# Blocks of four rows per partition for w2, the bias added on VectorE, and the tail rows of w2 on the load queue

## The chip, the cores and the metric

The kernel runs on one core of a Trainium2 chip. The metric is device time in microseconds (us), the median of several executions.

The engines go by their names in the profile: PE is TensorE's matmul and PEld its weight load, DVE is VectorE, ACT ScalarE, POOL GpSimd, and SP is SyncE, which issues most of the loads. The DMA engines carry a load in packets; it has *landed* when its semaphore, a counter that others wait on, has counted all of it. SBUF is the on-chip memory, 128 partitions, into which the loads write.

Two kinds of number appear. *Times* come from unprofiled executions, with a 95% interval on the ratio to the kernel before, run on the same chip. *Trace numbers* come from one profiled execution of each kernel; its span is about 2 us shorter than the time. A trace number has no interval, so differences of 0.2 us between two traces are not read as anything. Packet durations, landings and addresses that stand in no profile view were counted from the packet and semaphore records of the traces and from the built programs.

## The reference

A decode step: one token for each of four sequences goes through attention over a cache of 4096 positions, then through a small MLP.

```python
# x [4,1,640]; k_cache, v_cache [4,32,4096,128]; wq [640,4096]; wo [4096,640]
# w1 [640,1728]; b1 [1728]; w2 [1728,640]; all bf16
h  = x + attention(layernorm(x), k_cache, v_cache, wq, wo)
t  = layernorm(h) @ w1 + b1
sp = log1p(exp(-abs(t))) + where(t > 0, t, 0)
out = h + (t * tanh(sp)) @ w2
```

The two caches are 268 MB of the 283 MB read. The MLP weights, which the change is about, are 4.4 MB.

## The kernel before

P is 128 partitions, D is 640, F is 1728. F is FM = 13 full blocks of 128 and FT = 64 rest rows. DC = 5 is the number of 128-blocks in D, N = 4 the sequences, FC = 14 the blocks of F with the rest, CG = 4. One pool of four slots of 32 KB per partition takes the whole stream in turn: wq, then 64 cache tiles of 4 MB (key and value tiles, alternating), then half of wo, then w1.

```python
consts = ctx.enter_context(tc.tile_pool(name="consts", bufs=1))
stream = ctx.enter_context(tc.tile_pool(name="stream", bufs=NSLOT))     # NSLOT = 4
...
def load_cache(store, src, i, nm, parts=1):
    hg, b = tiles[i]
    t = stream.tile([P, SLOT], BF16, tag="s", name=f"{nm}{i}")          # SLOT = 16384: 32 KB
    view = src[b, hg * G : (hg + 1) * G].rearrange("h (q r) d -> (h q) (r d)", q=PG)
    n = SLOT // parts
    for k in range(parts):
        nc.sync.dma_start(out=t[:, k * n : (k + 1) * n], in_=view[:, k * n : (k + 1) * n])
...
w2_sb = consts.tile([P, FM, D], BF16)
W1S = (0, 2, 4, DC)
W2S = (0, 5, 10, FM)
def load_mlp():
    w1_slot = stream.tile([P, SLOT], BF16, tag="s", name="w1_slot")
    ...                                     # w1 in three loads, by W1S
    w2_v = B_w2[0 : FM * P, :].rearrange("(p j) n -> p j n", j=FM)      # partition p has rows 13p..13p+12
    for j0, j1 in zip(W2S, W2S[1:]):
        nc.sync.dma_start(out=w2_sb[:, j0:j1, :], in_=w2_v[:, j0:j1, :])
...
b1T = consts.tile([P, FM + 1], BF16)
nc.scalar.dma_start(out=b1T[:, 0:FM], in_=B_b1[0 : FM * P].rearrange("(p j) -> p j", j=FM))
nc.scalar.dma_start(out=b1T[0:FT, FM : FM + 1], in_=B_b1[FM * P : F].rearrange("(p o) -> p o", o=1))
...
ident_f = consts.tile([P, P], FP32)         # 512 bytes a partition
...
if i == 0:                                  # in the loop over cache tiles: the tail rows, mid-stream
    nc.scalar.dma_start(out=w2_tail[0:FT, :], in_=B_w2[FM * P : F, :])
    nc.scalar.dma_start(out=w2_tail[FT : FT + CG, :], in_=B_w2[F - CG : F, :])
...
b1s = consts.tile([P, FC, N], FP32)         # b1 times std; 224 bytes a partition
...
for c0, c1 in zip(W1S, W1S[1:]):
    if c1 == DC:                            # the bias, by an fp32 matmul with the identity
        nc.tensor.matmul(h1_ps[:, :, :], lhsT=ident_f[:, :], rhs=b1s[:, :, :], start=False, stop=False)
    for j in [FM] + list(range(FM)):
        for c in range(c0, c1):
            # column j of w1 for partition p is column 13p + j: 13 columns, 26 bytes, apart
            ...
            nc.tensor.matmul(h1_ps[0 : (P if j < FM else FT), j, :], lhsT=w, rhs=cen[:, c, :], ...)
# h1 = h1_ps * rstd, mish on ScalarE and VectorE -> act; then act @ w2_sb and act @ w2_tail
```

A weight tile of w1 is the stationary operand, so its columns are read by the weight load (PEld in the profile). The order in which rows of w2 lie on the partitions sets which columns of w1 must be read together: 13 apart here.

The softmax here doesn't subtract the row's maximum and nothing guards it: scores larger than these inputs give would overflow.

## Time and profile before

| | before |
|---|---|
| time, median of the first 3 runs | 670.02 us (669.18 to 670.12) |
| span in the trace | 667.5 us |
| last wo part landed | 652.61 |
| last w2 part landed | 662.96 |
| last w2 matmul done | 664.34 |

The page's slices: 40 equal parts of the span, first the busy share of the DMA engines in tenths, then what they moved; the third line counts packets.

```profile
DMA  9999999999999999999999999999999999999995
GB/s 376 440 411 438 419 438 435 432 427 439 432 427 430 430 436 429 438 437 423 432 437 431 433 428 436 437 430 427 434 437 436 429 429 432 438 431 430 427 415 241
DMA packets 12591, 283.81 MB, mean 425 GB/s; under 512 B 1608, under 2 KB 1680, under 8 KB 3728
```

The load stream is the limit in 39 of 40 slices. PE is busy 64% and VectorE 62% of the span, so both have time to spare. Two stretches of the stream, as windows (start and end in us, length, then busy time of PE, PEld, DVE, ACT and POOL with the instruction counts, granted TensorE clock, DMA share, GB/s):

```profile
100.00:300.00 200.00, 128.60 (x890) 59.66 (x889) 127.29 (x134) 20.50 (x93) 0.00 (x0) 0.82 1.00 432
300.00:500.00 200.00, 130.28 (x828) 59.01 (x827) 129.01 (x138) 20.56 (x96) 0.00 (x0) 0.83 1.00 432
```

Only in the last 11 us, after 656.86, does the chain stop waiting for loads. The chain of waits that ended last (start, length, what; the trace prints w1's slot as w_slot, w2_sb as w_sb, the product of w1 as h_ps, that of w2 as y_ps):

```profile
641.55 15.31 DMA w_slot<-in_B_w_dram
656.86 0.04 issue
656.90 1.89 PE h_ps L537 x28
658.80 0.52 PE h_ps L528 x2
659.32 1.02 PE h_ps L537 x14
...
661.91 0.23 DVE act L576
662.14 0.04 issue
662.18 2.16 PE y_ps L585 x55
664.34 0.02 issue
664.37 0.33 DVE o_bf L591
```

After the second part of w1 has landed (656.86) the chain runs through 28 w1 matmuls in 1.89 us, the fp32 bias matmul in 0.52 us (L528), 14 more, the activation, and 55 w2 matmuls. From the timeline (start, length, engine, line, operation, and in brackets the idle time before):

```profile
656.90 1.81 PEld L537 LDWEIGHTS <-w_slot 128*64 128x64 bf16 x28 [0.28 <-DMA w_slot<-in_B_w_dram]
662.41 1.91 PE L585 MATMUL y_ps<-w_sb,act 128*4 128x160 bf16 x52
```

A group of 28 w1 matmuls is paced by its weight loads: 1.81 us of 1.89. The w2 matmuls run without a wait. In all, PE is 1.4 us behind the last load.

### The profile page before, as it was taken

To read this page: it belongs to the slowest core of one execution; us is meant where nothing else is said; L and a number is where in the kernel's file an instruction comes from. 1 tells how busy PE (TensorE), PEld (TensorE's weight loads), DVE (VectorE), ACT (ScalarE), POOL (GpSimd) and SP (SyncE) were. 2 spreads that over 40 slices of the span, in tenths; PEclk is the share of its full clock that TensorE was granted. 3 is DMA by queue.
4 is the path that set the end of the run, shared out by engine and by line. 5 is a ranking of instruction groups with operands and counts; after the bars stand their busy time and mean duration, and the time that the engine had idled before them with its cause. 6 is when DMAs were issued, how large, how long until landed. Compare 5 with 4: busy or idle time off the path is not lost.

```text
span 667.5 us, 6967 instructions
## 1 busy us (share of the span) xinstructions
PE 426.0 (64%) x2937; PEld 198.2 (30%) x2937; DVE 411.7 (62%) x477; ACT 75.5 (11%) x312; POOL 1.9 (0%) x9
## 2 busy tenths in 40 slices
PE   1967546694567675574764865568765657747586
PEld 0323222242223332232332422233322223323145
DVE  3387565686565676465675666557765657757542
ACT  0401001010001110011100110101100111001011
POOL 1000000000000000000000000000000000000000
PEclk9987789897788976788877788979867898778895
DMA  9999999999999999999999999999999999999995
GB/s 376 440 411 438 419 438 435 432 427 439 432 427 430 430 436 429 438 437 423 432 437 431 433 428 436 437 430 427 434 437 436 429 429 432 438 431 430 427 415 241
DMA packets 12591, 283.81 MB, mean 425 GB/s; under 512 B 1608, under 2 KB 1680, under 8 KB 3728
## 3 DMA queue, kind: packets, MB, share of 16 engines
q1 hardware_dynamic: 12224, 283.27, 98.8%
q8 instruction: 23, 0.38, 0.2%
q10 hardware_dynamic: 336, 0.10, 0.1%
q14 instruction: 8, 0.07, 0.0%
HBM read 283.36 MB, written 0.01 MB: 424 GB/s over the span
## 4 chain that ended last, share of the span: by engine, by line
DMA 61%; DVE 19%; PE 18%; issue 1%; ACT 0%; SPq 0%; DVEq 0%; ACTq 0%
DVE prod L284 16%; PE red L296 14%; DMA k_1005<-in_A_k_cache_dram 4%; DMA k_530<-in_A_k_cache_dram 4%; DMA k_1480<-in_A_k_cache_dram 4%; DMA k_1955<-in_A_k_cache_dram 4%; DMA k_2881<-in_A_k_cache_dram 4%; DMA k_2428<-in_A_k_cache_dram 4%; DMA k_3334<-in_A_k_cache_dram 4%; DMA k_1691<-in_A_k_cache_dram 4%; DMA k_310<-in_A_k_cache_dram 4%; DMA k_3092<-in_A_k_cache_dram 4%; DMA k_1216<-in_A_k_cache_dram 3%; DMA k_741<-in_A_k_cache_dram 3%; DMA v_3666<-in_A_v_cache_dram 3%; DMA k_2166<-in_A_k_cache_dram 3%
## 5 line engine op out<-in xcount | busy, mean ns | idle before, releaser
L296 PE MATMUL red<-prod,ident 128*128 128x512 bf16 x1024 | 300.1, 451 | 218.9 <-DVE prod L284 218.0
L296 PEld LDWEIGHTS <-ident 128*128 128x128 bf16 x1024 | 116.0, 114 | 385.2 <-issue 317.6
L313 DVE TENSOR_REDUCE s_f<-red 128x32 f32<-128x512 f32 x128 | 88.1, 688 | 79.4 <-PE red L296 79.2
L316 ACT ACTIVATE ex<-s_f 128x32 bf16<-128x32 f32 x128 | 29.3, 229 | 516.6 <-DVE s_f L313 516.6
L323 DVE TENSOR_TENSOR e<-ex,hmask 128x128 bf16<-128x128 bf16 x128 | 36.5, 285 | 6.1 <-ACT ex L316 6.1
L373 PEld LDWEIGHTS o_ps<-selo,pv_sb 128*128 128x128 f32 x256 | 34.0, 194 | 6.0 <-ACT pv_sb L363 1.2
L352 PEld LDWEIGHTS <-e 128*16 128x16 bf16 x1024 | 22.6, 89 | 36.8 <-issue 15.5
L373 PE MATMUL o_ps<-selo,pv_sb 128*128 128x4 f32 x256 | 31.1, 245 | 0.7 <-ACT pv_sb L363 0.7
L316 ACT ACTIVATION_READ_ACCUMULATOR ex<-s_f 128x1 f32 x128 | 23.9, 187 | 0.1
L284 DVE TENSOR_TENSOR prod<-k_79,qbc 128x4096 bf16<-128x4096 bf16 x4 | 9.1, 2287 | 17.6 <-DMA k_79<-in_A_k_cache_dram 17.6
L379 DVE TENSOR_TENSOR OT<-o_ps,rl 128x16 bf16<-128x16 f32 x8 | 1.6, 195 | 21.0 <-PE o_ps L373 21.0
L256 PE MATMUL q_ps<-wq_74,lnT 128*4 128x512 bf16 x32 | 10.7, 470 | 4.7 <-DMA wq_74<-in_A_wq_dram 4.7
L284 DVE TENSOR_TENSOR prod<-k_1691,qbc 128x4096 bf16<-128x4096 bf16 x4 | 9.1, 2286 | 5.7 <-DMA k_1691<-in_A_k_cache_dram 5.7
L284 DVE TENSOR_TENSOR prod<-k_3092,qbc 128x4096 bf16<-128x4096 bf16 x4 | 9.1, 2286 | 5.7 <-DMA k_3092<-in_A_k_cache_dram 5.7
L284 DVE TENSOR_TENSOR prod<-k_1216,qbc 128x4096 bf16<-128x4096 bf16 x4 | 9.1, 2286 | 4.9 <-DMA k_1216<-in_A_k_cache_dram 4.9
L284 DVE TENSOR_TENSOR prod<-k_3545,qbc 128x4096 bf16<-128x4096 bf16 x4 | 9.1, 2286 | 4.9 <-DMA k_3545<-in_A_k_cache_dram 4.9
L284 DVE TENSOR_TENSOR prod<-k_741,qbc 128x4096 bf16<-128x4096 bf16 x4 | 9.1, 2285 | 4.9 <-DMA k_741<-in_A_k_cache_dram 4.9
L284 DVE TENSOR_TENSOR prod<-k_903,qbc 128x4096 bf16<-128x4096 bf16 x4 | 9.1, 2287 | 4.8 <-DMA k_903<-in_A_k_cache_dram 4.8
L284 DVE TENSOR_TENSOR prod<-k_428,qbc 128x4096 bf16<-128x4096 bf16 x4 | 9.1, 2286 | 4.6 <-DMA k_428<-in_A_k_cache_dram 4.6
L284 DVE TENSOR_TENSOR prod<-k_1378,qbc 128x4096 bf16<-128x4096 bf16 x4 | 9.1, 2286 | 4.5 <-DMA k_1378<-in_A_k_cache_dram 4.5
L284 DVE TENSOR_TENSOR prod<-k_1853,qbc 128x4096 bf16<-128x4096 bf16 x4 | 9.1, 2286 | 4.5 <-DMA k_1853<-in_A_k_cache_dram 4.5
L284 DVE TENSOR_TENSOR prod<-k_530,qbc 128x4096 bf16<-128x4096 bf16 x4 | 9.1, 2285 | 4.4 <-DMA k_530<-in_A_k_cache_dram 4.4
(179 smaller groups left out, 376.2 us busy)
## 6 DMA issues: line engine op xcount, KB each, us to landing
wq_74<-in_A_wq_dram SPq DMA_DIRECT2D x1, 4096.0 KB
k_79<-in_A_k_cache_dram SPq DMA_DIRECT2D x1, 4096.0 KB, 24.8
k_81<-in_A_k_cache_dram SPq DMA_DIRECT2D x1, 4096.0 KB, 33.9
v_83<-in_A_v_cache_dram SPq DMA_DIRECT2D x1, 4096.0 KB, 17.3
k_244<-in_A_k_cache_dram SPq DMA_DIRECT2D x1, 4096.0 KB
v_246<-in_A_v_cache_dram SPq DMA_DIRECT2D x1, 4096.0 KB
k_310<-in_A_k_cache_dram SPq DMA_DIRECT2D x1, 4096.0 KB, 24.6
v_314<-in_A_v_cache_dram SPq DMA_DIRECT2D x1, 4096.0 KB, 32.1
```

What stands on the lines that cost most here:

```text
L256: nc.tensor.matmul(q_ps[:, :], lhsT=lnT[:, c, :], rhs=wq_t[c // WQC][:, o : o + 512], start=(c == 0), stop=(c == DC - 1),)
L284: nc.vector.tensor_tensor(out=t[:, :, :], in0=kt[i][:, s * RS : (s + 1) * RS, :], in1=q_bc[hg][:, b, :].unsqueeze(1).to_broadcast([P, RS, ...
L296: nc.tensor.matmul(red[:, :, :], lhsT=ident[:, :], rhs=t[:, :, c * CW : (c + 1) * CW], start=(c == 0), stop=(c == Dh // CW - 1),)
L313: nc.vector.tensor_reduce(out=s_t[i][:, sl], in_=reds.pop((i, s))[:, :, :], axis=AX.X, op=ALU.add)
L316: nc.scalar.activation(out=ex_t[i][:, sl], in_=s_t[i][:, sl], func=ACT.Exp, scale=SCALE, accum_out=rs_t[hg][:, b, s : s + 1],)
L323: nc.vector.tensor_tensor(out=e_t[i][:, sl, :], in0=ex_t[i][:, sl].unsqueeze(2).to_broadcast([P, RS, G]), in1=hmask[:, :].unsqueeze(1).to_ ...
L352: nc.tensor.matmul(pvs[i % 2][k * QD : k * QD + RQ * G, :], lhsT=e_t[i][:, u * RQ : (u + 1) * RQ, :], rhs=vt[i][:, u * RQ : (u + 1) * RQ, ...
L373: nc.tensor.matmul(o_ps[hg][:, b, :], lhsT=t[:, r, :], rhs=selo[:, r, :], start=(r == 0), stop=(r == RQ - 1),)
L379: nc.vector.tensor_tensor(out=OT[:, hg * G : (hg + 1) * G, :].rearrange("p g b -> p b g"), in0=o_ps.pop(hg)[:, :, :], in1=rl.pop(hg)[:, :] ...
```

## The change

The intent is to shorten this last stretch. Rows of w2 go in blocks of four per partition, so that the w1 columns read together are 4 apart (8 bytes) and no longer 13 (26 bytes). b1 is added by VectorE after the product, so the fp32 matmul, its identity and its scaled operand go. The tail rows of w2 leave the middle of the stream and go on the load queue, in two pieces, right before w2. b1 has to follow the new order and becomes five small loads. The core of the diff:

```diff
-    W2S = (0, 5, 10, FM)
+    JW = 4
+    EB = 8
+    def fcols(t, j):
+        if j == FM:
+            return t[:, FM * P : F]
+        j0 = j - j % JW
+        w = min(JW, FM - j0)
+        return t[:, j0 * P : (j0 + w) * P].rearrange("k (p r) -> k r p", r=w)[:, j - j0, :]
...
-        for j0, j1 in zip(W2S, W2S[1:]):
-            nc.sync.dma_start(out=w2_sb[:, j0:j1, :], in_=w2_v[:, j0:j1, :])
+        for r0, r1 in ((0, FT - EB), (FT - EB, FT)):
+            nc.sync.dma_start(out=w2_tail[r0:r1, :], in_=B_w2[FM * P + r0 : FM * P + r1, :])
+        for j in range(0, FM, JW):
+            w = min(JW, FM - j)
+            nc.sync.dma_start(out=w2_sb[:, j : j + w, :],
+                in_=B_w2[j * P : (j + w) * P, :].rearrange("(p r) n -> p r n", r=w))
...
-    nc.scalar.dma_start(out=b1T[:, 0:FM], in_=B_b1[0 : FM * P].rearrange("(p j) -> p j", j=FM))
+    for j in range(0, FM, JW):
+        w = min(JW, FM - j)
+        nc.scalar.dma_start(out=b1T[:, j : j + w],
+            in_=B_b1[j * P : (j + w) * P].rearrange("(p r) -> p r", r=w))
...
-    ident_f = consts.tile([P, P], FP32)
-    nc.vector.tensor_copy(out=ident_f[:, :], in_=ident[:, :])
...
-        if i == 0:                 # both tail loads of the cache loop go
-            ...
-    b1s = consts.tile([P, FC, N], FP32)
-    ...                            # its multiply and the fp32 matmul go
-                    h1_ps[0 : (P if j < FM else FT), j, :], lhsT=w, rhs=cen[:, c, :],
+                    h1_ps[0 : (P if j < FM else FT), j, :],
+                    lhsT=fcols(w1_sb[:, c, :], j), rhs=cen[:, c, :],
...
+    nc.vector.tensor_tensor(
+        out=h1[:, :, :], in0=h1[:, :, :],
+        in1=b1T[:, :].unsqueeze(2).to_broadcast([P, FC, N]), op=ALU.add,
+    )
```

## The prediction

> **What bounds the kernel now.** The load stream. The page's slices show the DMA engines at 9 tenths in 39 of 40 slices, 425 GB/s over 283.8 MB; DVE is 62% busy, PE 64%. The landing events in the trace follow each other every 9.66 us per 4 MB cache tile from 64 us to the end, so what shifts the stream early shifts the end. The change leaves these bytes alone: only the last 15 us and some tenths elsewhere are at stake.
>
> **The last 15 us (timeline, chain of waits).** The last output-projection weights land at 652.61. The first group of w1 matmuls starts at 654.79 (after the centred input), the second at 656.90 (its w1 landed 656.86), 28 in 1.9 us each; the third part of w1 lands at 657.90, but PE gets to it only at 659.25, after group two and the fp32 bias matmul (0.52 us on the chain). w1 product done 660.34, activation 662.13, w2 matmuls 2.16 us to 664.34. The last w2 part lands at 662.96, so loads are only 1.4 us ahead of PE.
>
> **Saved.**
> 1. w1 column stride. Successive weight loads start 60 ns apart at a 26-byte stride, 40 ns at the 10-byte stride of the first transposition, 27 ns for contiguous columns. The Trainium skill, "SBUF — State Buffer", section on the DMA port swizzle, says that SBUF has 16-byte lines and each new line costs; the three spacings agree (128, 80, 16 lines). At 8 bytes (64 lines) I estimate 30 ns: a group of 28 takes about 1.0 us.
> 2. The bias matmul goes; a DVE add of about 0.25 us comes in after the w1 product.
>
> Group two then ends near 657.9, group three waits for its DMA at 657.90 and ends about 658.4: 1.9 us earlier, less 0.25. Activation done near 660.5.
>
> **What eats it.** PE reaches w2 columns 8 to 11 before that piece has landed; the last piece (1,280-byte rows, 55 ns a packet; 196 ns for 5,120) lands at about 663.3 if nothing else moves. PE would end near 663.7: a gain of 0.6 us.
>
> **Moved.** The w2 tail rows (4 packets of 55 ns per engine) leave the middle of the stream, where between 44 and 57 us two tiles took 10.45 and 9.99 us instead of 9.66: up to 0.9 us off; at the end they cost about 0.25. b1 becomes four small loads of 128 descriptors (before: one), 9 ns a packet, 24 more per engine: about 0.25 us. Splitting the tail 56 + 8 leaves two engines free of it (The Trainium skill, "DMA: Bandwidth & Descriptors", section on why a DMA increments its semaphore by 16; no view here shows engine numbers). Net: 0 to 0.5 us gained.
>
> **Sum.** About 1.0 us less: 669.0 us, range 667.8 to 670.4. Faster by over 2%: 0.01; within 2%: 0.98; slower: 0.01.
>
> **Right or wrong shows in:** w1 weight loads about 30 ns apart, first group about 1.0 us; PE idle before the third w1 group and a late w2 group, released by DMA; the chain ending in w2's last landing; tiles between 36 and 57 us at 9.7 to 9.9 us.
>
> **What would make it wrong.** An 8-byte stride costs as much as 26; the small b1 loads hold a semaphore that a cache load or the first square root waits for, and a bubble opens near 30 us; instruction fetches (16 KB; the spread of landings jumps from 1.9 to 3.4 and 3.2 to 4.7 us near two of them) fall differently on the slowest engine.

## The result

| | before | after |
|---|---|---|
| time, median of 6 | 669.59 us (669.18 to 670.12) | 672.41 us (672.24 to 672.71) |
| span in the trace | 667.5 | 670.5 |
| last wo part landed | 652.61 | 656.10 |
| last w2 part landed | 662.96 | 666.94 |
| last w2 matmul done | 664.34 | 667.42 |

The ratio is 1.0042, with a 95% interval of 1.0029 to 1.0055. (A ratio here and below is the mean time of one kernel's fast runs over the mean of the other's in the same rounds, so it is not quite the ratio of the medians.) That is within 2%, as predicted, but the sign is wrong, and 672.41 lies outside the predicted range.

The change is about the end of the kernel, and there it did its work: from the landing of the last wo part to the last w2 matmul, before took 664.34 - 652.61 = 11.73 us and after 667.42 - 656.10 = 11.32. But wo landed 3.49 us *later*, at a point that no changed instruction of the MLP has reached. The page of after:

```profile
DMA  9999999999999999999999999999999999999996
GB/s 374 434 408 434 419 436 432 432 423 437 426 429 430 426 436 426 436 431 425 431 431 427 435 428 432 425 432 437 426 433 426 433 437 423 432 428 436 425 406 255
DMA packets 13165, 283.81 MB, mean 423 GB/s; under 512 B 2058, under 2 KB 2254, under 8 KB 4302
```

The same windows of after:

```profile
100.00:300.00 200.00, 131.26 (x886) 60.50 (x885) 126.13 (x133) 20.51 (x93) 0.00 (x0) 0.83 1.00 430
300.00:500.00 200.00, 129.99 (x818) 58.11 (x816) 127.77 (x136) 20.25 (x94) 0.00 (x0) 0.83 1.00 430
```

The DMA share is 1.00 in both kernels, so there is no bubble: the engines are as busy and move less, 430 GB/s in place of 432. Both kernels load the same cache tiles here with the same instructions. The digits are coarse; the trace's packet records are finer. Durations of the 32 KB packets of the load queue between 100 and 600 us:

```
before   1213 ns x6489 of 6524                      mean 1214.7
after    1216 ns x3584, 1224 ns x1408, 1215 x612    mean 1219.7
```

In before nearly every packet takes exactly 1213 ns. In after hardly one does. A 4 MB tile lands every 9.66 us in before and every 9.72 us in after, and 0.05 to 0.06 us on each of some 59 tiles after the first five is about 3 us.

At the end the chain of after reads:

```profile
639.81 16.29 DMA wo_late<-in_A_wo_dram
656.10 0.02 issue
656.12 10.42 DMA w_sb<-in_B_w_dram
666.53 0.04 issue
666.57 0.86 PE y_ps L589 x15
667.44 0.02 issue
667.46 0.33 DVE o_bf L595
```

It goes through w2's landing, as the prediction said it would: PE is no longer behind the loads. And the timeline of after:

```profile
658.30 1.11 PEld L536 LDWEIGHTS <-w_slot 128*64 128x64 bf16 x28 [0.27 <-DMA w_slot<-in_B_w_dram]
660.59 1.78 PEld L536 LDWEIGHTS <-w_slot 128*64 128x64 bf16 x42 [1.18 <-DMA w_slot<-in_B_w_dram]
662.74 0.22 DVE L567 TENSOR_TENSOR h_4147<-h_4147,b1T 128x56 f32<-128x56 f32 x1
666.57 0.84 PE L589 MATMUL y_ps<-w_sb,act 128*4 128x160 bf16 x20 [0.55 <-DMA w_sb<-in_B_w_dram]
```

28 weight loads take 1.11 us where they took 1.81; the added VectorE instruction costs 0.22; PE waits 0.55 us for the last of w2.

So there are two questions: why does an untouched stream move 0.5% slower, and what became of the gains the prediction had summed up?

### The profile page after: what moved, and what is told of

It reads as the page before. It is cut to its first block, busy times and chain, and to the rows that moved or that the text cites. A ratio compares the mean times of both kernels' runs of the same rounds, so it can differ in the third digit from the quotient of the medians.

```text
span 670.5 us, 6968 instructions
## 1 busy us (share of the span) xinstructions
PE 429.9 (64%) x2935; PEld 198.2 (30%) x2935; DVE 410.9 (61%) x476; ACT 75.5 (11%) x312; POOL 1.9 (0%) x9
## 4 chain that ended last, share of the span: by engine, by line
DMA 64%; DVE 19%; PE 16%; issue 0%; ACT 0%; DVEq 0%
DVE prod L301 16%; PE red L313 14%; DMA k_1004<-in_A_k_cache_dram 4%; DMA k_1479<-in_A_k_cache_dram 4%; DMA k_529<-in_A_k_cache_dram 4%; DMA k_1954<-in_A_k_cache_dram 4%; DMA k_2880<-in_A_k_cache_dram 4%; DMA k_2427<-in_A_k_cache_dram 4%; DMA k_3333<-in_A_k_cache_dram 4%; DMA k_309<-in_A_k_cache_dram 4%; DMA v_3546<-in_A_v_cache_dram 4%; DMA k_3091<-in_A_k_cache_dram 4%; DMA k_1690<-in_A_k_cache_dram 4%; DMA k_79<-in_A_k_cache_dram 4%; DMA k_2165<-in_A_k_cache_dram 3%; DMA k_1215<-in_A_k_cache_dram 3%
## 5 line engine op out<-in xcount | busy, mean ns | idle before, releaser
L313 PE MATMUL red<-prod,ident 128*128 128x512 bf16 x1024 | 306.4, 459 | 215.7 <-DVE prod L301 214.7
L313 PEld LDWEIGHTS <-ident 128*128 128x128 bf16 x1024 | 117.9, 116 | 385.8 <-issue 321.2
```

Of the source, the lines that this page charges most:

```text
L313: nc.tensor.matmul(red[:, :, :], lhsT=ident[:, :], rhs=t[:, :, c * CW : (c + 1) * CW], start=(c == 0), stop=(c == Dh // CW - 1),)
```

## The experiments

What the change could have done to the whole stream: it removed two scratch tiles, `ident_f` (512 bytes a partition) and `b1s` (224), from the pool of constants that lies below the stream's slots. The addresses in the built programs:

```
before         slots start at 57600 = 225 * 256
after          slots start at 56864 = 222 * 256 + 32     (736 bytes lower)
```

**ADDRESS**: the slots' start, no longer a multiple of some power of two, slows every large packet. **BIAS**, the rival: the five small b1 loads in place of two disturb the stream, by a semaphore or a queue state that lasts. The expectations name a third theory, **TAIL**: the tail rows on the other queue in mid-stream had kept the stream of before out of the slow pattern. It falls with before_pad32, which keeps them there and is slow, and with after_pad224, which does not and is fast. Each experiment below changes the kernel named and is compared with before on the same chip.

### A. The start address

**A1. 32 bytes of padding in the kernel before** (and, A2, in the kernel after). The pad is a tile that nothing reads.

```diff
     w2_tail = consts.tile([P, D], BF16)
+    pad = consts.tile([P, 16], BF16, name="pad")
+    nc.gpsimd.memset(pad[:, :], 0.0)
```

Expected of the kernel before with the pad:

> The kernel before with nothing but a 32-byte tile put among the constants, so that the stream buffers start 32 bytes off a multiple of 64. ADDRESS: packets 1216 to 1224 ns, a cache tile every 9.72 us, about 3.5 us slower: 673 us. BIAS and TAIL: 1213 ns and 669.6 us.

Measured: 673.23 us (673.06 to 673.42), ratio 1.0053 (1.0038 to 1.0068). Its windows:

```profile
100.00:300.00 200.00, 130.07 (x886) 60.17 (x885) 126.14 (x133) 20.52 (x93) 0.00 (x0) 0.84 1.00 430
300.00:500.00 200.00, 129.32 (x818) 57.80 (x817) 127.76 (x136) 20.25 (x94) 0.00 (x0) 0.84 1.00 430
```

430 GB/s, and the packets are those of after: 1216 ns x3595, 1224 ns x1401, mean 1219.7. The kernel before, with nothing of the change in it, is made slow by 32 bytes that no one reads. This alone is larger than the whole result.

Expected of the kernel after with the pad:

> The changed kernel is slower because every 32 KB packet of the load stream takes 1216 to 1224 ns from about 75 us on, against 1213 ns before. Theory ADDRESS: taking away two scratch tiles moved the stream buffers from a start that is a multiple of 64 bytes to one that is 32 off; a pad of 32 bytes puts it back: packets 1213 ns to the end, a cache tile every 9.66 us, 668.5 to 669.5 us, so about 1 us under the kernel before. Theory BIAS (the four small b1 loads put the stream into the slow pattern) and theory TAIL (the tail rows on the second queue at 40 us had kept it out of it): no difference, 1216 to 1224 ns, 672.4 us.

Measured: 671.79 us (671.73 to 671.82), ratio 1.0031 (1.0016 to 1.0046). A miss for a unit of 64 bytes: the slots start at 56896, 64 above a multiple of 256, and the stream is still slow (mean packet 1218.7 ns).

**A3 and A4. The unit.** The same pad, of 96 and of 224 bytes, placed before `b1T`: the slots start 128 bytes above a multiple of 256, and on one.

> The same with 96 bytes: start at a multiple of 128 but not of 256. If 256 bytes is the unit: packets still 1215 to 1222 ns, 671.5 to 672 us. If 128 bytes is enough: 1213 ns and 668.4 to 669.2 us.

> The whole change, with 224 bytes of padding so that the stream buffers start at a multiple of 256 bytes (as in the kernel before; the change as it came starts them 32 above one, the 32-byte pad 64 above one). ADDRESS with a 256-byte unit: packets 1213 ns to the end, a tile every 9.66 us, and the shorter end of the kernel shows: 668.4 to 669.2 us, about 0.9 us under the kernel before. If no address decides it but something else that the change moved: 1215 to 1224 ns and 671.8 to 672.4 us.

| kernel | slots start, modulo 256 | 32 KB packets, mean (ns) | last wo landed | time | ratio to before |
|---|---|---|---|---|---|
| before | 0 | 1214.7 | 652.61 | 669.59 | 1 |
| after | 32 | 1219.7 | 656.10 | 672.41 | 1.0042 |
| before_pad32 | 32 | 1219.7 | 656.32 | 673.23 | 1.0053 |
| after_pad32 | 64 | 1218.7 | 655.61 | 671.79 | 1.0031 |
| after_pad96 | 128 | 1218.4 | 655.26 | 671.49 | 1.0030 (1.0015 to 1.0045) |
| after_pad224 | 0 | 1214.6 | 652.93 | 669.01 | 0.9992 (0.9980 to 1.0005) |

Of the starts tried, only the multiples of 256 are fast. With 224 bytes of padding the kernel after has 1213 ns in 6486 packets again, and its windows are:

```profile
100.00:300.00 200.00, 130.26 (x881) 60.05 (x880) 124.99 (x133) 20.51 (x93) 0.00 (x0) 0.82 1.00 432
300.00:500.00 200.00, 130.94 (x838) 59.82 (x836) 131.17 (x139) 20.48 (x96) 0.00 (x0) 0.83 1.00 432
```

432 is back, and the last wo part lands 3.17 us earlier than in after. The rest of the change is the same instructions.

**A5 and A6. Is it the destination of the loads, or the pool's place as such?** A pad moves everything allocated after it. So here no tile moves by less than 256 bytes: the slots are made 256 bytes longer and the cache tiles are written 32 bytes into their slot, once both caches, once only the value cache.

```diff
-        t = stream.tile([P, SLOT], BF16, tag="s", name=f"{nm}{i}")
+        ts = stream.tile([P, SLOT + 128], BF16, tag="s", name=f"{nm}{i}")
+        o = {"k": 16, "v": 16}[nm]          # second run: {"k": 0, "v": 16}
+        t = ts[:, o : o + SLOT]
```

> The kernel before with stream slots 256 bytes longer, and each key and value tile written 32 bytes into its slot; every other tile (products, scores, weights) keeps its alignment. If the start of the written run is what counts: packets 1216 to 1224 ns, a tile every 9.72 us, 672.5 to 673.3 us, as with the 32-byte pad. If the alignment of some other tile that the pad moved counts: 1213 ns and 669.6 us.

> The same for the value tiles alone. If each written run pays for itself: half the packets slow, key tiles 9.66 us and value tiles 9.72 us apart, about 671.4 us. If one misaligned stream slows all: 672.5 to 673.3 us.

Measured: 672.61 us, ratio 1.0048 (1.0033 to 1.0062), for both; 670.61 us, ratio 1.0018 (1.0005 to 1.0031), for the values alone, less than the 671.4 us expected. In the second trace key tiles land every 9.66 us and value tiles every 9.72: each tile is slow by its own address. The dose agrees in kind only: with half of the tiles off, the loss against before's median in the same call is 1.26 us of 3.26. A rival would be the engines, which read the shifted tiles too. The same trace speaks against it: the matmuls that read value tiles run in 22 of the 31 intervals that end in a key tile's landing (those with a load of wo in between left out), and the median of these intervals is 9.66 us with them and without; that of the value tiles' intervals is 9.72 with them and without. That leaves the SBUF address to which a packet is written as the cause.

The Trainium skill, "DMA: Bandwidth & Descriptors", section "How a descriptor splits into AXI transactions", says that a transaction has to begin on a 256-byte boundary and that a descriptor that doesn't pays for a partial first one; it speaks of reads. If the same held for writes, a 32 KB packet would touch 129 pieces of 256 bytes in place of 128, an estimate of +0.8% from that page if each piece cost the same; counted in the page's beats of 32 bytes it would be 1025 in place of 1024, an estimate of +0.1%, and more for a start 128 bytes off. The runs show +0.41% on the mean packet (1219.7 over 1214.7) and +0.6% on the distance between tiles (9.72 over 9.66). The unit agrees with the page. The mechanism was not tested: the size is nearer to the count of pieces than to that of beats, and it does not grow with the offset (1219.7, 1218.7 and 1218.4 ns at 32, 64 and 128 bytes).

One thing stays open here. By the packet durations the slowness sets in late: in after at about 75 us, while the first short packets of wo (5,120 bytes) pass; in before_pad32 at about 50 us, while the tail's 1,280-byte packets do. Before that, where no small packets pass, nearly all packets to the same kind of address take 1213 ns. The landings say otherwise. By the mean of a tile's 16 landings the second cache tile, at about 35 us, comes 9.72 us after the first in before_pad32, cache_off32 and after_b1_one, and 9.66 after it in before and in tail_moved (C3 below). In after the tiles that land between 45 and 65 us are 9.72 apart, in after_pad224 9.67 and 9.70. So the landings, for which the kernel waits, show the cost from the first tiles on, and the durations show only part of it: 8 packets of 5.0 ns more are 0.04 us of the 0.06 on a tile. Why the two records differ early is not settled by any run.

### B. The b1 loads

**B1. The kernel before with four b1 loads in the old order**, the column groups of the change but pieces 26 bytes apart in memory, and **B2, the kernel after with b1 loaded as before** (one load; a wrong bias order, relative error 0.043).

```diff
 # B1
-    nc.scalar.dma_start(out=b1T[:, 0:FM], in_=B_b1[0 : FM * P].rearrange("(p j) -> p j", j=FM))
+    for j in range(0, FM, 4):
+        w = min(4, FM - j)
+        nc.scalar.dma_start(out=b1T[:, j : j + w],
+            in_=B_b1[0 : FM * P].rearrange("(p j) -> p j", j=FM)[:, j : j + w])
```

> The kernel before with b1 in four small loads (right result, addresses as before). BIAS: packets 1216 to 1224 ns, about 673 us. ADDRESS and TAIL: packets 1213 ns; only the cost of 24 more tiny packets an engine, 0 to 0.4 us: 669.6 to 670.0 us. The second cache load is held back to about 13.9 us by its semaphore in all three, with no bubble after it.

> The changed kernel with b1 in one load in the old order (wrong b1 order on purpose; the result is nearly right since b1 is small). BIAS: packets 1213 ns, about 669 us. ADDRESS and TAIL: still 1216 to 1224 ns, 672.0 to 672.5 us.

Measured: B1 669.44 us, ratio 0.9996 (0.9979 to 1.0012). B2 671.94 us, ratio 1.0034 (1.0019 to 1.0049). BIAS falls: four loads don't slow the kernel before, and one load doesn't heal the kernel after.

**B3. The order of the pieces.** B1 kept the old order on purpose, so that the result stays right; that hid something. In B3 the kernel before takes b1's loads exactly as the change has them (wrong bias order, relative error 0.040).

> The kernel before with the four b1 loads exactly as the change has them (wrong b1 order on purpose). If the order of these loads in memory costs 0.8 us: landing of the fifth cache tile on the first engine near 65.1 us against 64.3, and 670.2 to 670.5 us. If not: as before_b1_four, 669.3 to 669.6 us.

Measured: 670.03 us (669.82 to 670.29), ratio 1.0009 (0.9996 to 1.0023), which alone decides nothing. The trace does. The fifth cache tile (first of its 16 engines) lands at 65.39 us, in B1 at 64.27; the last wo part at 653.66, in B1 at 652.78. The windows of B1, then of B3:

```profile
26.00:46.00 20.00, 13.97 (x56) 5.50 (x55) 16.64 (x14) 4.83 (x13) 0.00 (x0) 0.87 1.00 424
```

```profile
26.00:46.00 20.00, 13.65 (x62) 5.55 (x61) 18.09 (x16) 5.10 (x15) 0.00 (x0) 1.00 0.96 405
```

19 GB/s less over 20 us are 0.38 MB, at 430 GB/s 0.9 us of stream. Here, other than in A, the engines' busy share falls too, to 0.96. The packet records show where: between 28 and 44 us an engine is without a packet of the load queue for 0.63 us on average in B3 and 0.11 in B1. Most of that is one gap near 34.8 us, where the packets in flight fall from 16 to 3. And the 32 KB packets that begin between 30 and 38 us take 1260 ns on average, in B1 1213. SyncE had issued the next cache load at 28.93 us in B3 and at 28.97 in B1, so the gap is not that of a load held back by a semaphore. The number of loads and of bytes is the same in B1 and B3; only where the pieces lie in memory differs.

**B4 and B5. Which of the loads.** The change's b1 has three loads of 8-byte pieces and a fourth of single 2-byte elements (block 12 has one row per partition). Between 14 and 24 us, while 8-byte packets run, B1 and B3 move the same (429.4 and 429.0 GB/s from the packet records); the loss falls into the time of the 2-byte packets, which run from 28 us on. So the edit was split in two: in B4 only the 8-byte loads have the new order, in B5 only the 2-byte load.

```diff
+    for j in range(0, FM, 4):
+        w = min(4, FM - j)
+        if w == 4:                                  # B4; in B5: if w != 4
+            src = B_b1[j * P : (j + w) * P].rearrange("(p r) -> p r", r=w)
+        else:
+            src = B_b1[0 : FM * P].rearrange("(p j) -> p j", j=FM)[:, j : j + w]
+        nc.scalar.dma_start(out=b1T[:, j : j + w], in_=src)
```

> The kernel before with b1 in four loads: the three 8-byte ones in the change's order (neighbouring partitions read neighbouring 8 bytes), the fourth, of single 2-byte elements, in the old order (26 bytes apart). Wrong bias order on purpose. Theory TWO: the cost of the change's b1 loads sits in the fourth load, whose 128 elements of 2 bytes lie side by side in memory: in the earlier traces the loss falls between 34 and 44 us, while the 2-byte packets run and the DMA engines' busy share falls to 0.96, and the stretch 14 to 24 us with most of the 8-byte packets runs at full rate in both orders. It expects no cost here: fifth cache tile first landing at 64.2 to 64.5, busy share 1.00 in 34:44. Rival EIGHT: any load with neighbouring pieces costs: fifth tile at 65.0 or later, the share below 0.98.

> The complement: the three 8-byte loads in the old order (26 bytes apart), only the fourth load, 128 elements of 2 bytes, in the change's order, side by side. Wrong bias order on purpose. Theory TWO expects the whole cost: fifth cache tile first landing at 65.1 to 65.5, busy share 0.96 to 0.97 in 34:44, time 0.5 to 0.9 us above the kernel of the other run. Rival EIGHT expects the fifth tile at 64.2 to 64.5.

Measured: B4 669.28 us (669.20 to 669.68), fifth tile at 64.54; B5 670.37 us (670.23 to 670.51), fifth tile at 65.39. (With one of 13 columns misplaced, B5's result still passed the comparison.) The windows of B4, then of B5:

```profile
26.00:46.00 20.00, 13.97 (x58) 5.49 (x57) 16.77 (x14) 5.44 (x14) 0.00 (x0) 0.91 1.01 431
```

```profile
26.00:46.00 20.00, 13.97 (x58) 5.47 (x56) 16.76 (x14) 5.10 (x14) 0.00 (x0) 0.91 0.98 405
```

The cost goes with the fourth load: 128 elements of 2 bytes that lie side by side in memory. All runs of B5 (670.23 to 670.51) lie above all of B4 (669.20 to 669.68), on one chip. In B5 an engine is without a load packet for 0.66 us between 28 and 44 us and the 32 KB packets begun between 30 and 38 us take 1298 ns; in B4 it is 0.10 us and 1213 ns. The same load with its elements 26 bytes apart shows no such gap. (B4's fifth tile is 0.27 us behind B1's, so a small cost of the 8-byte loads is not excluded.) Two details missed: the fifth tile of B4 came 0.04 us after the expected range, and in B5 the busy share, counted from the packet records cut at the window's edges, was 0.97 in the stretch 24 to 34 us and 0.99 in 34 to 44 (the view, which counts a packet where it begins, has 0.98 and 0.95), so the loss began earlier than expected. Why neighbouring elements are slow stays open; the remaining 64 elements of b1, also side by side, are loaded the same way in every one of these kernels, before included.

### C. The parts that were meant to gain

Three kernels do one part alone, all with the slots on a multiple of 256. **C1**: only the bias on VectorE (`ident_f`, `b1s` and the fp32 matmul go, 224 bytes of padding come in). **C2**: only the blocks of four for w2, w1 and b1; bias matmul and tail as before. **C3**: only the tail rows moved:

```diff
         w2_v = B_w2[0 : FM * P, :].rearrange("(p j) n -> p j n", j=FM)
+        for r0, r1 in ((0, FT - 8), (FT - 8, FT)):
+            nc.sync.dma_start(out=w2_tail[r0:r1, :], in_=B_w2[FM * P + r0 : FM * P + r1, :])
...
-        if i == 0:
-            nc.scalar.dma_start(out=w2_tail[0:FT, :], in_=B_w2[FM * P : F, :])
-            nc.scalar.dma_start(out=w2_tail[FT : FT + CG, :], in_=B_w2[F - CG : F, :])
```

> The kernel before with b1 added on VectorE alone, padded so that the buffers start at a multiple of 256. The fp32 matmul was 0.52 us on the chain, the add is about 0.25: 0.2 to 0.4 us less, 669.2 to 669.4 us, packets 1213 ns.

> The kernel before with the blocks of four alone (w2, w1 columns and the four b1 loads), bias matmul and tail as before, addresses as before. From the changed kernel's own trace the first w1 group takes 1.2 us in place of 1.9; the bias matmul then stands in the chain after the last w1 part landed: activation done about 1.0 us earlier, w2 landing as before: 0.6 to 0.9 us less, 668.7 to 669.1 us. If the end of the stream decides more than I think: 669.3 us or more.

> The kernel before with the tail rows of w2 on the load queue in two pieces, ahead of w2, and nothing else of the change. My prediction: leaving the middle of the stream gives back up to 0.9 us there and costs 0.25 at the end, so 669.0 to 669.6 us. What the padded run of the change shows: no gain in the middle, 0.37 us in the landing of the last w2 piece; the w2 matmuls here end 1.4 us after that landing, so the time would be 669.4 to 669.8 us, all the same as before within its spread.

| kernel | time | ratio to before | last wo landed | from there to the last w2 landing | to the last w2 matmul |
|---|---|---|---|---|---|
| before (trace of the first page) | 669.59 | 1 | 652.61 | 10.35 | 11.73 |
| C1, bias | 669.58 | 1.0001 (0.9989 to 1.0014) | 653.06 | 10.33 | 11.49 |
| C2, blocks | 669.16 | 0.9996 (0.9984 to 1.0009) | 653.49 | 10.39 | 10.89 |
| C3, tail | 668.66 | 0.9991 (0.9979 to 1.0003) | 651.83 | 10.81 | 11.86 |
| after_pad224 | 669.01 | 0.9992 (0.9980 to 1.0005) | 652.93 | 10.74 | 11.26 |

None of the three is told from before by its time, and C1 and C3 missed what was expected (669.58 us for 669.2 to 669.4, 668.66 for 669.0 to 669.8; C2 lies just above its 668.7 to 669.1). The traces show where each gain and cost sits. C1 takes 0.24 us off the end. C2 takes 0.84 off the end, until PE waits for the last of w2, and its b1 loads cost 0.88 in the stream (that is B3's difference, and C2's wo lands within 0.2 us of B3's). C3 brings wo 0.78 us earlier and makes w2 land 0.46 later relative to it. Where PE is behind the loads anyway, that costs only 0.13; in the full change, where PE waits for w2, 11.26 - 10.89 = 0.37. The stretch that the tail used to disturb, in before and then in C3:

```profile
40.00:56.00 16.00, 11.91 (x80) 5.07 (x80) 12.67 (x14) 2.05 (x11) 0.00 (x0) 0.89 1.03 428
```

```profile
40.00:56.00 16.00, 11.90 (x80) 5.09 (x80) 12.43 (x13) 2.46 (x10) 0.00 (x0) 0.89 1.00 433
```

### D. Versions that might beat both

**D1 and D2.** The change, aligned, with the tail back on the other queue in mid-stream (one load) and w2's loads in another order, the small last block first, so that less is left to do after the last landing. Two pads, not printed, bring the slots, w2 and its tail to multiples of 256. The program was run twice.

```diff
-        for j in range(0, FM, JW):
+        for j0, j1 in ((12, 13), (0, 4), (4, 8), (8, 10), (10, 12)):
...                                  # the loads by these ranges; block 12 first in the w2 matmuls too
```

> The change, stream buffers and w2 at multiples of 256 bytes, the tail rows back on the second queue in the middle of the stream (without the unused four rows), the one-column piece of w2 loaded first and the last block cut in two pieces of two columns. The end then waits for the last landing and 8 matmuls in place of 20: last landing 0.3 to 0.4 us earlier, PE done 0.3 us after it: 668.2 to 668.8 us against 669.0 for the padded change.

> The same program as aligned_w2_order, for its two kinds of run. If the slow kind is the slow packets of the misaligned stream, a trace of it shows 1216 to 1224 ns; if it is a bubble, packets of 1213 ns and a gap somewhere; if all runs are near 669, the slow ones stay unexplained.

Measured: 669.03, 668.89, 672.04, 669.24, 672.81 and 672.65 us in the first; 672.10, 669.05, 669.12 and 669.45 in the second. The ratios, 1.0020 (1.0000 to 1.0039) and 1.0008 (0.9990 to 1.0025), are means over two kinds of run, 669 and 672, of one program; the granted clock, 0.822 to 0.830 in the slow kind and 0.824 to 0.839 in the other, does not tell them apart. Even the good kind misses the 668.2 to 668.8 us expected. The second profile caught the slow kind. The windows of the good and of the slow profile:

```profile
46.00:78.00 32.00, 19.94 (x141) 8.93 (x140) 20.17 (x22) 4.01 (x17) 0.00 (x0) 0.87 1.01 431
```

```profile
46.00:78.00 32.00, 22.84 (x146) 9.75 (x145) 20.34 (x22) 4.33 (x19) 0.00 (x0) 0.82 1.00 386
```

In the slow kind most 32 KB packets take 1353 to 1361 ns from about 46 us, as the tail's packets pass, until about 78, as the first short wo packets pass; then 1213 again. Three tiles land 10.8 to 10.9 us apart. What triggers it is not settled. It begins with the tail's packets, but before has a tail in mid-stream too, and none of its runs was of that kind. The tail of before is written to an address 128 above a multiple of 256, that of D1 to a multiple; no run separates this from the other differences.

**D3 and D4.** The change, aligned, with its tail on the load queue, and b1 loaded as one contiguous row into one partition and spread over the partitions by 14 small matmuls at the start, while PE is idle. D4 has w2's loads in the order of D1 as well.

```diff
-    for j in range(0, FM, JW):                   # and the load of the rest
-        ...
+    pad = consts.tile([P, 48], BF16, name="pad")
+    b1_row = consts.tile([1, F], BF16)
+    nc.scalar.dma_start(out=b1_row[:, :], in_=B_b1.rearrange("(o f) -> o f", o=1))
...
+    b1_ps = ps.tile([P, FM + 1], FP32, tag="misc", name="b1_ps")
+    for j in range(FM + 1):
+        nc.tensor.matmul(b1_ps[0 : (P if j < FM else FT), j : j + 1],
+            lhsT=fcols(b1_row[:, :], j), rhs=ident[0:1, 0:1], start=True, stop=True)
+    # two copies from b1_ps to b1T
```

> The change, buffers at multiples of 256, with b1 loaded as one row and spread over the partitions by 14 small matmuls at the start, so that none of the tiny b1 writes goes through the load stream. If these cost 0.8 us: the first engine's third value and key landings come 0.8 us earlier than in the padded change (landing of the fifth cache tile near 63.6 us against 64.4), 668.0 to 668.4 us. If they cost the 0.25 I predicted: 668.7 to 669.0 us.

> The same with the one-column piece of w2 first and the last block in two pieces of two columns: 8 instead of 20 matmuls after the last wait: 0.2 to 0.4 us less than aligned_b1_row, 667.7 to 668.2 us. If it shows the two kinds of run of aligned_w2_order, the order of the w2 loads is what brings them.

Measured: D3 668.09 us (667.79 to 668.40), ratio 0.9980 (0.9967 to 0.9993); D4 667.92 us (667.87 to 668.14), ratio 0.9978 (0.9965 to 0.9992). Both are correct. In D3 the fifth tile lands at 63.29 us, in after_pad224, which differs in how b1 comes in, at 64.39 (in before at 64.32, and in C3, whose tail has left mid-stream too, at 63.52). The chain of D4:

```profile
655.92 6.50 DMA w_sb<-in_B_w_dram
662.43 0.04 issue
662.47 0.47 PE y_ps L594 x8
662.93 0.02 issue
```

w2 has landed at 662.43, and only 8 matmuls are left. D4 beats before by 0.2%, with the interval clear of 1, and after by 4.5 us in the medians. The difference between D3 and D4 is not resolved.

## Why the prediction was wrong

**The step that failed**: "The change leaves these bytes alone: only the last 15 us and some tenths elsewhere are at stake." The bytes and the instructions were left alone; their destination was not. Two scratch tiles fewer moved the slots from a multiple of 256 to 32 bytes above one, and each 32 KB packet of the stream took 1219.7 ns on average in place of 1214.7. Of the 3.49 us by which the last wo part lands later, 3.17 go away with 224 bytes of padding. The prediction had the right premise, "what shifts the stream early shifts the end", and didn't ask what a removed tile does to the addresses of the tiles behind it. Its list of what could make it wrong hasn't it either.

The rest, point by point:

1. *w1 column stride: 30 ns a weight load, about 1.0 us for a group of 28.* Right: weight loads start 60 ns apart in before and 32 to 33 ns in after. A group of 28 took 1.19 us in after_pad224. This agrees with the Trainium skill, "SBUF — State Buffer", section on the DMA port swizzle, whose remark on 16-byte lines the estimate rested on.
2. *The bias.* Right: the 0.52 us matmul went, a VectorE add of 0.22 us came in, and the net in C1 is 0.24 us.
3. *Activation done 1.65 us earlier.* In after_pad224 it was done 1.28 us earlier, relative to the last wo part.
4. *PE then waits for loads, and the net at the end is 0.6 us.* Right in kind: the third group waits for w1 and the last for w2, and the chain ends in w2's landing. The net was 0.41 us in after and 0.47 in after_pad224.
5. *The tail: up to 0.9 us off in mid-stream, 0.25 on at the end.* Measured 0.78 (C3) and 0.13 to 0.37. The two pieces use 14 and 8 engines: their landings count 15 and 9 increments, one for each engine and one for all that are not used. That is what the Trainium skill, "DMA: Bandwidth & Descriptors", section "Why a DMA increments its semaphore by 16 and not by 1", leads one to expect.
6. *Four small b1 loads: 0.25 us, by counting packets.* Mis-sized: 0.88 us, and not for the number of loads (B1: none) but for the one load of 2-byte elements side by side (B5). A bubble did open, near 35 us, but not by a semaphore, as the prediction's list had it. It took back what the moved tail gave.

The sum with these sizes, and no misalignment: -0.78 + 0.88 - 0.47 = -0.37 us. The measured time of after_pad224 is 0.9992 of before's, -0.5 us, with an interval of -1.3 to +0.3. So the predicted gain of 1.0 us lies within that interval, but it is not shown; b1 cost 0.63 us more than forecast. The lateness of wo in after_pad224, 0.32 us, is 0.10 by this sum; the other 0.2 us is left unexplained, and is no more than traces of one kernel differ.

## What to carry to other kernels

When a kernel is bound by a load stream, look at the addresses of its buffers first: a change that adds or removes a tile allocated below them can move them off a multiple of 256 bytes, and this one lost 0.5% of the whole run, more than its intended gain, until 224 bytes of padding put it right. If a stretch that the change doesn't touch has become slower at the same DMA share, compare the spacing of landings and the packet durations there before arguing about the part that was edited. Load a short vector as one contiguous row and spread it on an engine that has time, rather than as hundreds of 2-byte packets beside a stream.

## What the Trainium skill lacked or had wrong

- "DMA: Bandwidth & Descriptors", section "How a descriptor splits into AXI transactions", has the 256-byte boundary for reads only. The runs show it for the SBUF address that a load writes to: starts 32, 64 and 128 bytes above a multiple of 256 cost 0.3 to 0.5% of the time (mean 32 KB packet 1218.4 to 1219.7 ns, against 1214.6 to 1214.7 at multiples of 256).
- No page says that this cost shows in the spacing of landings before it shows in packet durations: in before_pad32 9.72 us against 9.66 at the second cache tile (about 35 us), while its 32 KB packets begun between 20 and 38 us take 1213 ns as those of before do.
- "DMA: Bandwidth & Descriptors", section "Why small descriptors are slow (HBM only)", gives small pieces a fixed overhead each and does not speak of where they lie. Here 128 elements of 2 bytes side by side in memory cost 0.6 to 0.9 us of a full stream (fifth tile at 65.39 against 64.54 us, last wo part at 653.62 against 653.01), and the same elements 26 bytes apart nothing that shows.
- No page has the second kind of run of D1 and D2: most 32 KB packets at 1353 to 1361 ns in place of 1213 for some 30 us (386 against 431 GB/s), worth 3 us.
